# The second product of an MLP's last two token chunks in seven block products of 128x256 instead of eight, after all of the first product

## The chip, the core and the metric

The kernel runs on one core of a Trainium2 chip. Its engines work side by side, each through its own list of instructions in order: TensorE (PE; its weight loads have a row of their own, PEld), VectorE (DVE), ScalarE (ACT), GpSimd (POOL) and SyncE (SP), which here issues nearly all transfers. The metric is the device time of one execution in microseconds, the median of three runs. Products go into eight banks of 128x512 f32 (PSUM); everything else lies in the core's on-chip memory (SBUF) or in the chip's DRAM.

## The reference, cut to what matters

Windowed attention over 8 batches of 8 heads gives x, 4608 tokens of 512 features; an MLP follows. Only the MLP is touched by the change:

```python
h = x @ w_in                                    # 4608x512 by 512x2048
sp = np.maximum(h, 0.0) + np.log1p(np.exp(-np.abs(h)))
g = h * erf(sp)
out = (g @ w_out).astype(np.float32)            # 4608x2048 by 2048x512
```

Every matrix product is made of three: each operand is split into a rounded part (hi) and the rest (lo), and hi by hi, hi by lo and lo by hi are added up in PSUM. Splitting an operand takes a cast (hi, on ACT or DVE) and a subtraction (lo, on DVE).

## The kernel before

The tokens go in nine chunks of 512, the 2048 features of h in eight pairs of 256 (`SPC` is 8, `PAIR` is 2). Chunks 0 to 2 are done plainly, one (chunk, pair) after the other, while most of the attention is still worked off. Chunks 3 to 8 are taken as three couples (`DOUBLES`): for a couple and a pair of features, that is for one d of 0 to 23, h is made by Strassen's seven block products (`mm1_big(d, k)`, k of 0 to 6, L768; six matmuls of 128x512 each, 42 for a d) and `take_big` (L776 to L788) adds each of them into four tiles of 128x512 on DVE: t0 is a copy, t1 to t4 and t6 are additions of 512 columns, t5 one of 1024. The two results of a d are A (the couple's first chunk) and B (its second). They need, in this order, softplus (`argument_big`, L801, ACT), erf (in `period`, L877, ACT) and the product with h (`multiply_big`, L805, DVE). softplus and erf need an ACT table load each time the function changes. B is written to DRAM (`kept_g`) and fetched again later by `load_g`.

The second product is made of items: an item is one chunk's 256 features, (A, d) or (B, d), 24 matmuls of 128x512 (`item_products`, run by `mm`, L636) that add into four banks, `acc`, one per 128 tokens. `split` (L611, L612) makes an item's hi and lo, in halves j of 0 and 1. After the eighth item of a chunk `store` copies the four banks out (L672) and writes them.

This work is laid out by hand in 50 periods, one item in each. In `ITEMS` the items of a couple stand as A of its eight d, then B of its eight d, two periods behind its products. Periods 0 to 7, 16 to 23 and 32 to 39 also hold the 42 products of a d (66 matmuls in all); the other periods have the item's 24 alone. In a period with a d the matmuls go: two block products, six matmuls of the item, two block products, six, two, six, one, six. The block products alternate between two banks, h and tx, so that one product waits until what was in its bank two products earlier has been taken; between the block products the item's matmuls cover that. The order in which an engine gets its instructions is that of the code in `period`; nothing reorders them. `AFT` is a table of small jobs, keyed by period and place (0 to 3) in it; in the periods without a d they build the right-hand sums (`LESS`, `HI`, `LO`) of the next couple. The transfers of a d's left-hand sums (`load_left`, 1.75 MB) alternate between two places in `win`.

## Time and profile before

| | |
|---|---|
| median of three runs | 891.42 us (891.29 to 893.15) |
| the profiled execution: time, span | 892.89 us, 890.9 us |
| granted TensorE clock, mean | 0.996 |
| busy: PE, PEld, DVE, ACT, POOL | 98%, 79%, 71%, 63%, 9% |
| first block product of d = 0, 8, 16 (periods 0, 16, 32) | 354.87, 540.81, 713.14 us |
| bytes moved by DMA | 170.41 MB, 191 GB/s over the span |

A row of a group names the line, the engine, the operation, what it writes and reads, the shape and the count; behind the first bar stand the busy time and the mean length of one in ns, behind the second the time that the engine sat idle just before them and what ended it. A timeline row gives start and length in us and, in brackets, the idle time before it and what ended that. A matmul's or a cast's length there is from its start to its end; the next one of the engine can start before that end. In what follows a "step" of the products of h is the 42 matmuls of one d.

### The profile page before, as it was taken

To read this page: it belongs to the slowest core of one execution; us is meant where nothing else is said; L and a number is where in the kernel's file an instruction comes from. 1 tells how busy PE (TensorE), PEld (TensorE's weight loads), DVE (VectorE), ACT (ScalarE), POOL (GpSimd) and SP (SyncE) were. 2 spreads that over 40 slices of the span, in tenths; PEclk is the share of its full clock that TensorE was granted. 3 is DMA by queue.
4 is the path that set the end of the run, shared out by engine and by line. 5 is a ranking of instruction groups with operands and counts; after the bars stand their busy time and mean duration, and the time that the engine had idled before them with its cause. 6 is when DMAs were issued, how large, how long until landed. Compare 5 with 4: busy or idle time off the path is not lost.

```text
span 890.9 us, 20870 instructions
## 1 busy us (share of the span) xinstructions
PE 871.2 (98%) x8134; PEld 700.1 (79%) x8134; DVE 633.6 (71%) x1575; ACT 564.5 (63%) x1271; POOL 81.3 (9%) x97
## 2 busy tenths in 40 slices
PE   7799999999999999999999999999999999999998
PEld 3367888888888888788887778888888888888886
DVE  5878888987798889777676765666566647576622
ACT  6889888897788886675677442774445434445321
POOL 2312201111111110011000000010000000000000
PEclk9999999999999999999999999999999999999999
DMA  8874446464658896566675741674449125442341
GB/s 272 295 245 154 128 155 197 148 232 127 222 203 270 295 341 248 172 224 221 204 239 200 272 176 54 209 237 161 166 155 361 51 83 200 166 154 83 140 144 48
DMA packets 66915, 170.41 MB, mean 191 GB/s; under 512 B 7680, under 2 KB 14592, under 8 KB 63744
## 3 DMA queue, kind: packets, MB, share of 16 engines
q1 hardware_dynamic: 66528, 168.55, 55.1%
q8 instruction: 64, 1.05, 0.5%
q10 hardware_dynamic: 288, 0.52, 0.2%
q14 instruction: 35, 0.29, 0.1%
HBM read 122.91 MB, written 46.14 MB: 190 GB/s over the span
## 4 chain that ended last, share of the span: by engine, by line
PE 91%; DVE 5%; DMA 1%; ACT 1%; issue 1%; POOL 1%; SPq 0%; DVEq 0%; POOLq 0%; ACTq 0%
PE acc L636 43%; PE h L768 13%; PE tx L768 13%; PE h L521 7%; PE tx L521 7%; PE sp L275 3%; PE sp L217 3%; PE sp L256 1%; PE h L357 1%; DMA qk<-in_qk_dram 1%; DMA v<-in_v_dram 1%; DVE w L458 0%; DVE w L459 0%; DVE prob L228 0%; DVE win L453 0%
## 5 line engine op out<-in xcount | busy, mean ns | idle before, releaser
L636 PE MATMUL acc<-wout_hi,ghi 128*128 128x512 f32 x576 | 227.4, 395 | 0.5 <-DVE ghi L611 0.4
L636 PE MATMUL acc<-wout_lo,ghi 128*128 128x512 f32 x576 | 224.6, 390 | 0.0
L636 PE MATMUL acc<-wout_hi,glo 128*128 128x512 f32 x576 | 159.0, 389 | 0.0
L636 PEld LDWEIGHTS acc<-wout_hi,ghi 128*128 128x128 f32 x576 | 108.2, 188 | 23.3 <-DVE ghi L611 0.9
L636 PEld LDWEIGHTS acc<-wout_hi,glo 128*128 128x128 f32 x576 | 108.1, 188 | 22.8
L636 PEld LDWEIGHTS acc<-wout_lo,ghi 128*128 128x128 f32 x576 | 108.2, 188 | 21.7
L251 POOL TENSOR_TENSOR prob<-prob,rinv 128x256 f32<-128x256 f32 x72 | 72.7, 1016 | 477.0 <-DVE ssum L249 239.9
L238 ACT ACTIVATE prob<-prob,nmax 128x64 f32<-128x64 f32 x288 | 96.3, 338 | 10.5 <-DVE nmax L228 10.3
L801 ACT ACT_TABLE_LOAD x24 | 30.8, 1283 | 93.0 <-DVE dbl L776 47.3
L768 PE MATMUL tx<-win 128*128 128x512 f32 x288 | 74.1, 392 | 0.8 <-DVE hc L778 0.8
L228 DVE CUSTOM_DVE_ANT_0 prob<-sp,cst 128x64 f32<-128x64 f32 x288 | 45.3, 220 | 40.6 <-ACT rows L317 28.2
L768 PE MATMUL h<-win 128*128 128x512 f32 x288 | 74.0, 392 | 0.0
L768 PEld LDWEIGHTS tx<-win 128*128 128x128 f32 x288 | 53.5, 188 | 12.7 <-DVE hc L778 1.2
L768 PEld LDWEIGHTS h<-win 128*128 128x128 f32 x288 | 53.4, 188 | 12.0 <-DVE dbl L778 0.8
L612 DVE TENSOR_TENSOR glo<-hc,ghi 128x512 fp32r<-128x512 f32 x50 | 34.5, 692 | 33.4 <-PE acc L636 22.6
L238 ACT ACTIVATION_READ_ACCUMULATOR prob<-prob,nmax 128x1 f32 x288 | 54.7, 190 | 0.0
L612 DVE TENSOR_TENSOR glo<-dbl,ghi 128x512 fp32r<-128x512 f32 x48 | 33.4, 696 | 28.3 <-PE acc L636 15.6
L521 PE MATMUL h<-x,win 128*128 128x512 f32 x192 | 48.8, 396 | 0.0
L877 ACT ACTIVATE s<-s 128x1024 f32<-128x1024 f32 x48 | 48.2, 1052 | 0.3
L521 PE MATMUL tx<-x,win 128*128 128x512 f32 x192 | 48.0, 392 | 0.0
L801 ACT ACTIVATE s<-hc 128x1024 f32<-128x1024 f32 x24 | 25.5, 1061 | 34.9 <-DVE hc L776 22.8
L611 ACT CAST ghi<-hc 128x512 fp32r<-128x512 f32 x24 | 14.9, 623 | 50.0 <-PE acc L636 41.9
...
## 6 DMA issues: line engine op xcount, KB each, us to landing
...
```

The source lines that it names most:

```text
L217: nc.tensor.matmul(sps[h][r * STRIP:(r + 1) * STRIP, i, p, :], qkz[i][hs, s * STRIP:(s + 1) * STRIP], qkz[i][hs, at:at + KEYS], start=True ...
L228: nc.vector.tensor_tensor_reduce(out=pr[:, g, :], in0=sps[h][:, u % 2, p, :], in1=mask[QUADS.index(kinds(u, p))], scale=-SCALE, scalar=HUG ...
L238: nc.scalar.activation(out=probs[u][:, j, :], in_=probs[u][:, j, :], func=AF.Exp, scale=-1.0, bias=nmax[:, j:j + 1], accum_out=sums[u][:, ...
L251: nc.gpsimd.tensor_tensor(probs[u], probs[u], rinv.broadcast_to([P, 2 * PARTS, KEYS]), op=ALU.mult)
L275: nc.tensor.matmul(xp[h * D:(h + 1) * D, qs], vt[ks, s, h, :], pt[ks, h * P + s * STRIP:h * P + (s + 1) * STRIP], start=True, stop=True, t ...
L521: nc.tensor.matmul((h, bank)[j], win_at[:, ftp, j, cc // 2, w, cc % 2, :], x[cc], start=(k == 0 and i == 0), stop=(k == CC - 1 and i == 2))
L611: (copy or nc.vector.tensor_copy)(out=ghi, in_=e)
L612: nc.vector.tensor_tensor(out=glo, in0=e, in1=ghi.bitcast(F32), op=ALU.subtract)
L636: nc.tensor.matmul(args["out"], args["lhsT"], args["rhs"], start=args["start"], stop=args["stop"])
L768: nc.tensor.matmul(bank_, w[:, wi, c, :], x[c][:, xi, :], start=(c == 0 and n == 0), stop=(c == 1 and n == 2))
L801: nc.scalar.activation(out=ls[kind_, d], in_=hs[kind_, d], func=AF.Softplus)
L877: nc.scalar.activation(out=e, in_=e, func=AF.Erf)
```

## The change

Three things change for the last couple (chunks 7 and 8, d of 16 to 23); everything before period 32 keeps its place.

**The last periods are replaced.** `ITEMS` ends with period 31; its two last items, (B, 14) and (B, 15), are set aside (`REST`). Then `final(d)` makes all of h of the couple, eight steps of 42 matmuls with nothing between them, in four banks (h, tx and the attention's two, sp). A step begins on ACT with both erf of the step before, and t0, the copy, goes to ACT; A is also written to DRAM now (`ga`). `rest_steps` does the two items that were set aside, with the last erf and the last products with h. Then 16 `sums_step`: for chunk 7 and then chunk 8, for each half of its tokens (256), for each quarter of the features (512), the second product is made as seven block products of 128x256: seven products of six matmuls, 42 for a step, that add over the four quarters into seven of the eight banks. After the last quarter `sums_out` adds the seven banks up to the four output blocks and writes them.

**The sums that this needs.** Of g: `row_sums` (four subtractions or additions of 256 columns on DVE) and `operands` (casts on ACT, lo on DVE), made two steps ahead. Of w_out: eight times, p of 0 to 7, `sub_whole` (hi plus lo, two operations of 512 columns on DVE), `sub_sums` (four of 256 columns on DVE, then two casts on ACT) and `sub_split` (two of 512 columns on DVE, four transfers to DRAM, `wd`). Those are put into `AFT` and `LATE`: p = 0 into period 9, p = 5 into periods 11, 13 and 15, p = 1, 2, 3 into periods 20, 21, 22, p = 4 into 23 and 25, p = 6 into 31 and the first step of `final`, p = 7 into its second to fourth. `load_sums` fetches them.

**Small moves.** The loads of the third couple's B11 and B21 go from place 0 of period 24 to its place 3, and in odd d the two tiles that A and B get are swapped.

The counts: 384 matmuls of 128x512 (16 items) become 672 of 128x256, and weights are loaded for each matmul, as before. PE's list has 4134 rows instead of 4150, DVE's 1680 instead of 1548.

```diff
+FIN = DOUBLES - 1
+QUART = SPC // 2
+LASTS = [(kind_, half, q) for kind_ in "AB" for half in range(2) for q in range(QUART)]
...
-        first, then = (("B11", "B21"), ("B12", "B22")) if k == 1 else (("B12", "B22", "B11", "B21"), ())
+        first, then = (("B11", "B21"), ("B12", "B22")) if k == 1 else (("B12", "B22"), ("B11", "B21"))
...
+    SUBS = [lambda p: sub_whole(p), lambda p: sub_sums(p), lambda p: sub_split(p)]
+    for p, places in ((0, ((9, 0), (9, 1), (9, 3))), (1, ((20, 1), (20, 2), (20, 3))), (2, ((21, 1), (21, 2), (21, 3))),
+                      (3, ((22, 1), (22, 2), (22, 3))), (4, ((23, 1), (23, 3), (25, 3))),
+                      (5, ((11, 0), (13, 0), (15, 0))), (6, ((31, 0), (31, 3)))):
+        for sub, (i, q) in zip(SUBS, places):
+            also(i, q, (sub, p))
...
-    ITEMS = [NT - 2, NT - 1] + [(kind_, i * SPC + k) for i in range(DOUBLES) for kind_ in "AB" for k in range(SPC)]
+    ITEMS = [NT - 2, NT - 1] + [(kind_, i * SPC + k) for i in range(FIN) for kind_ in "AB" for k in range(SPC)]
+    ITEMS, REST = ITEMS[:-2], ITEMS[-2:]
+
+    def bank_of(d, k):
+        return (h, bank, *spb)[(7 * d + k) % (4 if d >= FIN * SPC else 2)]
...
         if k == 0:
-            nc.vector.tensor_copy(out=a[:, 1], in_=y)
+            (nc.scalar.copy if d >= FIN * SPC else nc.vector.tensor_copy)(out=a[:, 1], in_=y)
...
-        if kind_ == "B":
-            nc.sync.dma_start(out=kept_g[d // SPC][d % SPC], in_=e)
+        if (kind_, d // SPC) in kept_g:
+            nc.sync.dma_start(out=kept_g[kind_, d // SPC][d % SPC], in_=e)
...
+    def sums_product(s, k):
+        q = s % QUART
+        y, (xh, xl) = bank_at(s, k), operand(s, k)
+        for j in range(2):
+            at_, (wh, wl) = slice(j * P, (j + 1) * P), right(2 * q + j)[k]
+            for n, (x, w) in enumerate(((xh, wh), (xh, wl), (xl, wh))):
+                nc.tensor.matmul(y, x[:, at_], w, start=(q == 0 and j == 0 and n == 0),
+                                 stop=(q == QUART - 1 and j == 1 and n == 2))
...
+    def final(d):
+
+        chain = d > FIN * SPC
+        if chain:
+            for kind_ in "AB":
+                e = ls[kind_, d - 1]
+                nc.scalar.activation(out=e, in_=e, func=AF.Erf)
+        for k in range(4):
+            mm1_big(d, k)
+            take_big(d, k)
+        load_left(NT + d + 2, 0)
+        if chain:
+            multiply_big("A", d - 1)
+        mm1_big(d, 4)
+        take_big(d, 4)
+        jobs(HALFWAY.get(d - FIN * SPC, ()))
+        argument_big("A", d)
+        if chain:
+            multiply_big("B", d - 1)
+        for k in (5, 6):
+            mm1_big(d, k)
+            take_big(d, k)
+        argument_big("B", d)
+        load_left(NT + d + 2, 1)
+        jobs(LATE.get(d - FIN * SPC, ()))
+
+    LATE = {0: [(sub_split, 6)], 1: [(sub_whole, 7)], 2: [(sub_sums, 7), (load_e, 0, room_halves)],
+            3: [(sub_split, 7)], 4: [(row_sums, 0, room_w)], 5: [(operands, 0, 0), (operands, 0, 1)],
+            6: [(operands, 0, 2), (operands, 0, 3), (load_rest,), (load_sums, 0), (load_sums, 1)],
+            7: [(load_e, 1, lambda: slab(1)), (load_sums, 2)]}
+    HALFWAY = {7: [(split_rest, 0, 0), (split_rest, 0, 1)]}
...
+    def sums_step(s):
+        last_ = s % QUART == QUART - 1
+        for g, ks in enumerate(GROUPS):
+            for k in ks:
+                sums_product(s, k)
+            if s == 0 and g == 0:
+                operands(1, 3)
+            if g == 0:
+                row_sums(s + 2, room_s)
+            if last_:
+                for k in ks:
+                    sums_out(s, k)
+            operands(s + 2, g)
+        load_e(s + 4, lambda: room_e(s + 4))
+        if s < 2:
+            load_sums(6 + s)
...
+        for d in range(FIN * SPC, DOUBLES * SPC):
+            final(d)
+        rest_steps()
+        for s in range(len(LASTS)):
+            sums_step(s)
```

How the lists of instructions change at three places (dbl_ and hc are tiles of h, s the tiles of softplus and erf; the new lines are those of the changed kernel). **ACT, from d = 18 to d = 19**, before and then after:

```order
L801 ACTIVATE s<-dbl_8622 128x1024
L801 ACTIVATE s<-dbl_8623 128x1024
L877 ACT_TABLE_LOAD
L877 ACTIVATE s<-s 128x1024 x2
L801 ACT_TABLE_LOAD
L801 ACTIVATE s<-hc 128x1024 x2
```

```order
L821 ACTIVATE s<-hc 128x1024 x2
L1135 ACT_TABLE_LOAD
L1135 ACTIVATE s<-s 128x1024 x2
L798 COPY dbl_8667<-sp_90 128x512
L821 ACT_TABLE_LOAD
L821 ACTIVATE s<-dbl_8667 128x1024
L821 ACTIVATE s<-dbl_8668 128x1024
```

The second list is from d = 17 to d = 18: the copy t0 of a new step (L798) now stands on ACT, behind the softplus and both erf of the step before. **DVE, the step d = 18 of the changed kernel**, which starts with t1:

```order
L796 TENSOR_TENSOR dbl_8667<-sp_91,dbl_8667 128x512
L796 TENSOR_TENSOR dbl_8668<-h,dbl_8667 128x512
L796 TENSOR_TENSOR dbl_8668<-tx,dbl_8668 128x512
L825 TENSOR_TENSOR hc<-hc,s 128x1024
L796 TENSOR_TENSOR dbl_8667<-sp_90,dbl_8668 128x512
L825 TENSOR_TENSOR hc<-hc,s 128x1024
L808 TENSOR_TENSOR dbl_8668<-sp_91,dbl_8668 128x1024
L796 TENSOR_TENSOR dbl_8668<-h,dbl_8668 128x512
```

The split of items (L616, L617), which stood among these rows, is gone; t1 reads the tile that ACT's copy wrote. **DVE, period 21 (d = 13)**, before and after:

```order
L778 COPY hc<-tx 128x512
L776 TENSOR_TENSOR hc<-h,hc 128x512
L776 TENSOR_TENSOR hc<-tx,hc 128x512
L776 TENSOR_TENSOR hc<-h,hc 128x512
L805 TENSOR_TENSOR dbl_7713<-dbl_7713,s 128x1024
L611 CAST ghi<-dbl_7713 128x512
L612 TENSOR_TENSOR glo<-dbl_7713,ghi 128x512
L776 TENSOR_TENSOR hc<-tx,hc 128x512
L788 TENSOR_TENSOR hc<-h,hc 128x1024
L805 TENSOR_TENSOR dbl_7714<-dbl_7714,s 128x1024
L776 TENSOR_TENSOR hc<-tx,hc 128x512
```

```order
L798 COPY hc<-tx 128x512
L796 TENSOR_TENSOR hc<-h,hc 128x512
L796 TENSOR_TENSOR hc<-tx,hc 128x512
L796 TENSOR_TENSOR hc<-h,hc 128x512
L950 TENSOR_TENSOR rows<-wout_hi,wout_lo 128x512 x2
L825 TENSOR_TENSOR dbl_7747<-dbl_7747,s 128x1024
L616 CAST ghi<-dbl_7747 128x512
L617 TENSOR_TENSOR glo<-dbl_7747,ghi 128x512
L950 TENSOR_TENSOR rows<-rows 128x256 x4
L796 TENSOR_TENSOR hc<-tx,hc 128x512
L808 TENSOR_TENSOR hc<-h,hc 128x1024
L825 TENSOR_TENSOR dbl_7748<-dbl_7748,s 128x1024
```

Six operations (L950) stand ahead of t4, which is the next to last L796 row. **DVE and ACT, period 9 of the changed kernel**, where chunk 3 ends and p = 0 is built:

```order
L617 TENSOR_TENSOR glo<-hc,ghi 128x512
L950 TENSOR_TENSOR s<-wout_hi,wout_lo 128x512 x2
L950 TENSOR_TENSOR s<-s 128x256 x4
L617 TENSOR_TENSOR glo<-dbl_6633,ghi 128x512
L677 COPY o<-acc_93 128x512
L677 COPY w<-acc_95 128x512
```

```order
L974 CAST s<-s 128x512 x2
L616 CAST ghi<-dbl_6633 128x512
L677 COPY w<-acc_94 128x512
L677 COPY w<-acc_96 128x512
L616 CAST ghi<-dbl_6633 128x512
```

The copies that free the banks acc (L677; L672 before) now stand behind the L950 rows on DVE and behind two casts of p's sums (L974) on ACT; before, neither was there.

More of the change, by code (lines that the diff above doesn't have):

```diff
@@ L771, in take_big @@
     def take_big(d, k):
-        y = (h, bank)[(7 * d + k) % 2]
+        y = bank_of(d, k)
         if k == 0:
@@ L794, in pair_of @@
         if d % 2:
-            return [work.tile([P, PAIR, TOK], F32, name="hc") for _ in range(2)]
+            return [work.tile([P, PAIR, TOK], F32, name="hc") for _ in range(2)][::-1]
         return [slab(i) for i in range(2)]
@@ new lines, in sub_whole, with sub_sums @@
+    def sub_whole(p):
+        subs[p] = sub_room(p)
+        for j, r in enumerate(subs[p][0]):
+            less(r, wout_hi[:, 2 * p + j, :].bitcast(F32), wout_lo[:, 2 * p + j, :].bitcast(F32), ALU.add)
+    def sub_sums(p):
+        (b11, b12), (b21, b22) = [(t[:, 0:HN], t[:, HN:TOK]) for t in subs[p][0]]
+        less(b11, b12, b11)
+        less(b12, b22, b12)
+        less(b22, b22, b11)
+        less(b21, b22, b21)
+        for r, hi in zip(*subs[p]):
+            nc.scalar.copy(out=hi, in_=r)
@@ new lines, in right, with load_e @@
+    def right(p):
+        w11, w12, w21, w22 = ([w[:, 2 * p + j, n * HN:(n + 1) * HN] for w in (wout_hi, wout_lo)]
+                              for j in range(2) for n in range(2))
+        return w11, w21, sum_at(p, 1, 1), sum_at(p, 0, 1), sum_at(p, 0, 0), w22, sum_at(p, 1, 0)
+    es, rs, ops = {}, {}, {}
+    GROUPS = ((0, 1), (2, 3), (4, 5), (6,))
+    def load_e(s, room):
+        if s < len(LASTS):
+            kind_, half, q = LASTS[s]
+            es[s] = room()
+            for k in range(2):
+                to = es[s][k] if isinstance(es[s], list) else es[s][:, k].rearrange("p (j n) -> p j n", j=PAIR)
+                nc.sync.dma_start(out=to,
+                                  in_=kept_g[kind_, FIN][2 * q + k][:, :, half * HN:(half + 1) * HN])
@@ new lines, in room_e, with parts_of, row_sums @@
+    def room_e(s):
+        return work.tile([P, PAIR, TOK], F32, name="hc") if s % 2 else slab(1 - s // 2 % 2)
+    def parts_of(s):
+        view = "p k (j r n) -> p k j r n"
+        if isinstance(es[s], list):
+            return [(slice(k, k + 1), t.rearrange("p (k j) (r n) -> p k j r n", k=1, r=2))
+                    for k, t in enumerate(es[s])]
+        return [(slice(0, 2), es[s].rearrange(view, j=PAIR, r=2))]
+    def row_sums(s, room):
+        if s < len(LASTS):
+            r = rs[s] = room()
+            for ks, e in parts_of(s):
+                a11, a12, a21, a22 = (e[:, :, j, n, :] for n in range(2) for j in range(PAIR))
+                s2, s3, s1, s4 = (t.rearrange("p (n k m) -> p n k m", n=2, k=2)[:, n, ks]
+                                  for t in r for n in range(2))
+                less(s1, a21, a22, ALU.add)
+                less(s2, s1, a11)
+                less(s3, a11, a21)
+                less(s4, a12, s2)
@@ new lines, in room_s, with op_room @@
+    def room_s():
+        t = work.tile([P, PAIR, TOK], F32, name="s")
+        return [t[:, 0], t[:, 1]]
+    def op_room(s):
+        if s % 2 == 0:
+            return [work.tile([P, S], F32R, name="rows", bufs=4)[:, 0:TOK] for _ in range(4)] + [
+                one.tile([P, QW + KW], F32R, name=f"qk{i}")[:, 0:TOK] for i in range(2)] + [
+                one.tile([P, TOK], F32R, name="v0")]
+        wide = [io.tile([P, PAIR, TOK], F32R, name=n, bufs=1) for n in ("plain", "dbl2")]
+        return [w[:, j] for w in wide for j in range(PAIR)] + [
+            one.tile([P, TOK], F32R, name="v1"), one.tile([P, TOK], F32R, name="pT1"),
+            work.tile([P, TOK], F32R, name="ghi")]
```

136 lines of the change are left out of this document (133 added, 3 removed).

## The prediction

> **What bounds the kernel now.** I read the page's busy times and its chain of waits first, then busy times by stretch, then timelines of single engines at the places that change.
>
> ```profile
> PE 871.2 (98%) x8134; PEld 700.1 (79%) x8134; DVE 633.6 (71%) x1575; ACT 564.5 (63%) x1271; POOL 81.3 (9%) x97
> ...
> PE 91%; DVE 5%; DMA 1%; ACT 1%; issue 1%; POOL 1%; SPq 0%; DVEq 0%; POOLq 0%; ACTq 0%
> ```
>
> The chain that ended last is PE for 91%: what counts is how many matmuls there are, at what pace, and where they wait. By stretch (engines' busy us, then granted clock, DMA share and GB/s):
>
> ```profile
> 497.30:502.00 4.70, 4.26 (x20) 3.22 (x18) 2.09 (x3) 3.75 (x4) 0.00 (x0) 1.00 0.99 363
> ...
> 609.64:654.60 44.96, 44.96 (x205) 37.25 (x199) 28.39 (x38) 20.44 (x25) 0.00 (x0) 1.00 0.46 160
> ...
> 713.14:832.80 119.66, 119.66 (x529) 99.10 (x528) 75.73 (x102) 51.60 (x49) 0.00 (x0) 1.00 0.38 132
> ```
>
> The last row covers the eight steps of h that the change rebuilds: PE is never idle there, and DVE (75.7 of 119.7) and ACT (51.6) have room, because each step also holds an item. The pace and the end, from PE's timeline (the last row is ACT's issue of a transfer):
>
> ```profile
> 873.62 0.39 PE L636 MATMUL acc<-wout_hi,ghi 128*128 128x512 f32 x1
> ...
> 876.34 0.39 PE L636 MATMUL acc<-wout_hi,ghi 128*128 128x512 f32 x1
> ...
> 886.99 0.39 PE L636 MATMUL acc<-wout_hi,glo 128*128 128x512 f32 x1
> ...
> 888.03 0.34 ACTq L674 DMA_DIRECT2D out_dram<-w  x1
> ```
>
> Twelve matmuls lie between the first two rows: 2.72 / 12 = 0.2267 us each. From 713.14 to the end there are 8 x 42 + 18 x 24 = 768 of them, 174.1 us, up to 887.25; the last copy and transfer take 3.65, which gives the span of 890.9. That stretch of 177.8 us is what I cost anew.
>
> **The products of 128x256.** They remove 384 matmuls (87.05 us) and add 672 of half the length, each with weights of its own. What weights cost shows where PE had stood still, and in the steady stream:
>
> ```profile
> 483.57 0.76 PEld L768 LDWEIGHTS tx<-win 128*128 128x128 f32 x4 [1.21 <-DVE hc L778]
> 483.57 0.96 PE L768 MATMUL tx<-win 128*128 128x512 f32 x3 [0.79 <-DVE hc L778]
> ...
> 879.06 0.39 PE L636 MATMUL acc<-wout_hi,ghi 128*128 128x512 f32 x1
> 879.06 0.19 PEld L636 LDWEIGHTS acc<-wout_lo,ghi 128*128 128x128 f32 x1
> ```
>
> Three matmuls after the stall took 0.96; 2 x 0.2267 + 0.39 is 0.84, so the first waited about 0.11 for its weights. In the stream a load starts together with the matmul before it (879.06), so it is hidden. Bounds for a matmul of 256 columns: half of 0.2267, 0.113, if the loads of 0.11 stay just hidden; 0.113 + 0.11 = 0.223, if nothing overlaps at this length. The stream's row is nearest to the lower one; I take 0.120, since no room is left over the loads. 672 x 0.120 = 80.6: **6.4 us less** (bounds 11 less, 63 more). The Trainium skill (TensorE: Matmul & The Clock Gate, Back-to-back issue gap) puts a lone matmul at its columns over 2.4 GHz plus 2.5 ns, 109 ns here; by that estimate the 672 take 73 us and the saving is 14. For 512 columns the same rule gives 216 ns where this trace shows 227, so I stay with the row.
>
> **The chain through final.** In a step PE needs 42 x 0.2267 = 9.52 us. But t0 is now ACT's, behind both erf of the step before; these wait for that step's softplus of B, this for its t6, and t6 stands last on DVE, behind the rest of the step. So ACT's stretch and DVE's follow one another. Before, the same pieces show at d = 15 (DVE, then ACT, then PE):
>
> ```profile
> 663.02 0.69 DVE L776 TENSOR_TENSOR hc<-tx,hc 128x512 f32<-128x512 f32 x1 [0.67 <-PE tx L768]
> 663.63 1.22 DVE L805 TENSOR_TENSOR dbl<-dbl,s 128x1024 f32<-128x1024 f32 x1
> 664.95 0.43 DVE L611 CAST ghi<-dbl 128x512 fp32r<-128x512 f32 x1
> ...
> 666.09 1.22 DVE L805 TENSOR_TENSOR dbl<-dbl,s 128x1024 f32<-128x1024 f32 x1
> 667.23 1.22 DVE L788 TENSOR_TENSOR hc<-h,hc 128x1024 f32<-128x1024 f32 x1
> 668.55 0.69 DVE L776 TENSOR_TENSOR hc<-tx,hc 128x512 f32<-128x512 f32 x1
> ...
> 672.80 1.22 DVE L805 TENSOR_TENSOR hc<-hc,s 128x1024 f32<-128x1024 f32 x1 [2.28 <-ACT s L877]
> ```
> ```profile
> 669.33 1.06 ACT L801 ACTIVATE s<-hc 128x1024 f32<-128x1024 f32 x1 [3.39 <-DVE hc L776]
> 670.41 1.28 ACT L877 ACT_TABLE_LOAD   x1
> 671.71 2.01 ACT L877 ACTIVATE s<-s 128x1024 f32<-128x1024 f32 x2
> ```
> ```profile
> 675.06 0.39 PE L636 MATMUL acc<-wout_hi,ghi 128*128 128x512 f32 x1
> ...
> L593 ACT COPY hc<-h 128x512 f32<-128x512 f32 x8 | 4.5, 566 | 0.0
> ...
> L611 ACT CAST ghi<-hc 128x512 fp32r<-128x512 f32 x24 | 14.9, 623 | 50.0 <-PE acc L636 41.9 <-DMA hc<-g 6.7 <-issue 1.4
> ```
>
> ACT's part: t6 ends at 669.24; softplus, table load and the two erf (started 0.95 apart) let the copy start at 673.6; with its 0.57 and, as from t6 to softplus, 0.09 to reach DVE that is 5.0 after t6. DVE's part: an operation of 512 columns lets the next start after 0.61 (663.02 to 663.63), one of 1024 after 1.14 (666.09 to 667.23); one that needs the result before it starts some 0.10 after its end (1.32 from 667.23 to 668.55). t1 0.61, t2 0.79, t3 0.61, product A 1.14, t4 0.61, product B 1.14, t5 1.32, t6 0.69: 6.9. A step takes **11.9 instead of 9.5**; there are seven such passages: 7 x 2.4 = 16.9 us. Four banks don't help: PE's fifth product waits for the bank that this copy empties, and PE stands still some 2.4 us per step.
>
> Jobs that lie in the chain: after d = 18 two casts on ACT wait for four small DVE operations (priced below: 1.8, then 1.2 for the casts, 1.1 of it hidden by softplus): 1.9. After d = 21 casts of 512 and twice 256 columns, 1.2, and after d = 22 of 512 and twice 128, 1.1 (estimates from the cast's 0.62). In d = 23 two lo's ahead of product B, 2 x 0.61 = 1.2. Together 5.4. The other jobs of LATE run on DVE while it waits for ACT, 5 us each time, and cost nothing; in a chain without that wait they would cost 1.2 to 2.4 each.
>
> Ends: t6 of the first step lies 0.9 behind PE (0.2 and 0.69). After the last t6, (B, 15) needs its hi, cast behind both erf: 5.1; then 24 matmuls, 5.44, with about 0.5 for its second half's lo, which stands behind two products of h: 11.0. Item (B, 14) fits into the wait.
>
> The sums: a step of 42 takes PE 5.04. DVE does about 1.5 for row_sums and 2.2 for lo's, made two steps ahead, and 4.2 more, nine additions, in each fourth step: 19.0 per four steps against PE's 20.2. ACT needs 2.3 of 5.04. I cost this at nothing; at the pace of 0.113 (19.0) DVE would just set it. Transfers: 2.75 MB per step of final over 11.9 us, 231 GB/s, and some 17 MB in the 90 us behind it, against 363 in the first stretch row: hidden.
>
> From 713.14: 76.2 + 0.9 + 16.9 + 5.4 + 11.0 + 80.6 + 3.65 = 194.7 instead of 177.8: **+16.9**.
>
> **The small jobs ahead of it.** What an operation of 256 columns costs, and period 21 (DVE; PE):
>
> ```profile
> 340.71 0.41 DVE L540 TENSOR_TENSOR dbl<-dbl 128x256 f32<-128x256 f32 x1
> 341.16 0.42 DVE L541 TENSOR_TENSOR dbl<-dbl 128x256 f32<-128x256 f32 x1
> 341.62 0.43 DVE L542 TENSOR_TENSOR dbl<-dbl 128x256 f32<-128x256 f32 x1
> ...
> 634.81 0.68 DVE L776 TENSOR_TENSOR hc<-tx,hc 128x512 f32<-128x512 f32 x1
> ```
> ```profile
> 636.98 0.84 PE L768 MATMUL tx<-dbl,win 128*128 128x512 f32 x3
> ```
>
> Four of 256 in a row take 4 x 0.46 = 1.84, two of 512 1.22. In period 21 all six stand ahead of t4 (634.81), which would end at 638.56; k6 needs t4's bank and was due at 636.98: 1.6 late, and the same in periods 20 and 22: 4.8. In period 23 t6 (668.55) comes 1.2 later, then sub_sums and two casts stand ahead of erf's table load on ACT: product A at 675.9 instead of 672.80, and its item on PE at 677.7 instead of 675.06: 2.6. Period 9:
>
> ```profile
> 504.29 0.69 DVE L612 TENSOR_TENSOR glo<-hc,ghi 128x512 fp32r<-128x512 f32 x1
> 505.08 0.69 DVE L612 TENSOR_TENSOR glo<-dbl,ghi 128x512 fp32r<-128x512 f32 x1
> 505.71 0.69 DVE L672 COPY o<-acc 128x512 f32<-128x512 f32 x1
> ```
> ```profile
> 507.55 0.39 PE L636 MATMUL acc<-wout_hi,ghi 128*128 128x512 f32 x1
> ...
> 524.00:529.50 5.50, 5.50 (x26) 4.53 (x26) 3.95 (x8) 1.73 (x4) 0.00 (x0) 1.00 0.43 161
> ```
>
> The sums end at 508.0, two casts on ACT at 508.7, the next item's hi behind them at 509.3, its lo at 510.1 and only then the copy that frees the first bank, at 510.7. PE wants that bank at 507.55: 3.2. p = 5 and 6 stand in periods of the last row's kind, DVE 3.95 of 5.50 us: nothing, about 1 each if that room is gone. Sum: **+10.6**.
>
> **The rivals.** (1) The small jobs are covered: DVE has 16.6 of 45 us free in periods 20 to 22 (second stretch row), more than the 3 x 4.28 = 12.8 that is added. Against it: in a list that is worked off in order the place decides, not the sum. 908. (2) Faster: ACT's and DVE's stretches overlap after all, so that a step ends within PE's 9.52; then 76.2 + 0.9 + 11.0 + 80.6 + 3.65 = 172.4, 5.4 less than before, 886 with the jobs covered. It decides, with all other jobs covered, from passages under 10.3 us on. Only each engine's own sum speaks for it (7 us per step on either); the copy's place behind the erf speaks against it. (3) Weights are not hidden at 256 columns: 672 x 0.223, 69 us more, 988. The loads' start with the matmul before speaks against it. (4) TensorE's clock falls in the gaps:
>
> ```profile
> 8.00:13.00 5.00, 2.90 (x41) 1.28 (x40) 1.97 (x11) 2.82 (x15) 0.83 (x2) 0.83 0.95 314
> ...
> 366.00:370.00 4.00, 2.47 (x14) 1.81 (x12) 3.34 (x7) 0.73 (x1) 0.00 (x0) 1.00 0.01 4
> ```
>
> Idle for 2.1 of 5 us the clock was 0.83, 0.85 us lost; idle for 1.5 of 4 it stayed 1.00. Within final PE has 2.4 us per step to lose; behind the 4.6 us before (B, 15) it hasn't: 1 to 2 us, 921. The Trainium skill (TensorE: Matmul & The Clock Gate, HAM oscillation) has the clock halve after an idle window of about 3.4 us; only that last gap and those behind the added casts are as long.
>
> **How the numbers follow.** 16.9 + 10.6 = 27.5: the profiled execution, 892.89 (span 890.9 and 2.0 around it), would become 920.4. The median lies 1.47 below it, 891.42, so I forecast **919**. Chances: this 0.66, (1) 0.15, (2) 0.08, (3) 0.03, (4) 0.05, and 0.03 that errors of both signs leave no change. Its own range is 912 to 925 (pace 0.113 takes 4.7 off, DVE-bound sums and 3 us of stalls add). With (1) at the lower pace 903, and with (4) and late transfers 927: 903 to 927. Some 0.2% is what a measurement of this kernel can tell from no change: faster 0.09, within it 0.03, slower 0.88.
>
> **What would show it.** In the changed profile: steps of L788 11.9 us apart with PE idle 2 to 4 us in each, behind ACT's L798; L1091 at 0.120 per matmul without gaps; PE waiting for DVE in period 9 (3 us), before k6 in 20 to 22, and in 25. Steps 9.5 us apart would prove the forecast wrong, and so would L1091 at 0.2.

## The result, and the profile after

The changed kernel takes **933.85 us** (median of 5 runs, 930.65 to 935.84) against 892.60 of the kernel before beside it (5 runs, 891.29 to 893.80): a ratio of **1.0463, 95% interval 1.0435 to 1.0491**. The forecast was 919, range 903 to 927: the direction was right, the time 7 us outside the range. The profiled execution took 930.65 (span 928.9), 37.8 more than the profiled one of before.

Busy times and the chain of waits, on the page after:

```profile
PE 875.0 (94%) x8410; PEld 714.3 (77%) x8422; DVE 698.8 (75%) x1747; ACT 601.7 (65%) x1347; POOL 80.1 (9%) x97
...
PE 75%; DVE 11%; ACT 5%; DMA 5%; issue 3%; POOL 0%; SPq 0%; DVEq 0%; ACTq 0%; POOLq 0%
```

PE's share of the chain fell from 91% to 75%; DVE, ACT and DMA took its place. By stretch of the changed kernel (from d = 12 to 15; d = 15 to 16; d = 16 to the first product of the sums; their first four steps; the other twelve), columns as in the prediction:

```profile
611.26:661.15 49.89, 45.91 (x205) 37.04 (x199) 38.15 (x59) 23.83 (x30) 0.00 (x0) 1.00 0.56 181
661.15:722.83 61.68, 59.40 (x259) 48.19 (x258) 46.38 (x74) 28.94 (x42) 0.00 (x0) 1.00 0.59 205
722.83:831.65 108.82, 92.70 (x385) 73.52 (x384) 68.14 (x98) 65.15 (x73) 0.00 (x0) 0.97 0.70 238
831.65:865.26 33.61, 24.86 (x170) 24.45 (x168) 19.36 (x48) 10.06 (x22) 0.00 (x0) 0.80 0.79 286
865.26:925.61 60.35, 60.35 (x506) 60.35 (x504) 45.69 (x103) 23.29 (x43) 0.00 (x0) 1.00 0.32 104
```

The last row is what was forecast for all of the sums: 504 products in 60.35 us, 0.120 each, PE never idle. The row above it was not: four steps, 168 products, 20.2 us at that pace, took 33.6, and the granted clock was 0.80. What PE waited for there, and further back in final (PE's waits from 800 on: us in total, times, longest):

```profile
PE sp L1091 <- DMA win<-wd: 8.7, 2, 6.5
PE acc L641 <- ACT ghi L616: 3.3, 1, 3.3
PE sp L788 <- ACT dbl L798: 3.2, 1, 3.2
PE tx L788 <- ACT hc L798: 1.3, 1, 1.3
```

The first row is a transfer: w_out's sums, loaded into win's cells, came late. SP's own list of issues shows why (start, time to issue; below them the wait of SP that stands in the gap, and count, size and median us to landing of these loads):

```profile
823.75 1.18 SPq L1007 DMA_DIRECT2D dbl<-ga  x2
825.02 1.02 SPq L987 DMA_DIRECT2D win<-wd  x2
827.49 0.32 SPq L828 DMA_DIRECT2D ga<-hc  x1
828.62 0.32 SPq L828 DMA_DIRECT2D g<-hc  x1
835.56 1.18 SPq L1007 DMA_DIRECT2D hc<-ga  x2
836.83 2.04 SPq L987 DMA_DIRECT2D win<-wd  x4
...
SPq L1007 <- DMA g<-hc: 6.6, 1, 6.6
...
win<-wd SPq DMA_DIRECT2D x16, 512.0 KB, 7.6
```
```profile
845.11 2.29 PE L1091 MATMUL sp<-win,dbl 128*128 128x256 f32 x9 [6.46 <-DMA win<-wd]
...
860.42 1.42 PE L1091 MATMUL sp<-win,dbl 128*128 128x256 f32 x9 [2.28 <-DMA win<-wd]
```

From 828.94 to 835.56 SP stood still: the left side of step 2 (L1007) goes into the buffer whose store (828.62) had not landed. The weights of p = 3 and 4 stand behind it and are issued at 836.83, 20 us after the last product of h (816.55), though their cells were empty by then; loads of this kind land a median 7.6 us after their issue. Step 1 wanted p = 3 at 838.6 and went on at 845.1 (PE's first row); step 3 waited in the same way for p = 7.

The chain through final went as forecast. DVE, ACT and PE around d = 18:

```profile
744.35 0.69 DVE L796 TENSOR_TENSOR hc<-tx,hc 128x512 f32<-128x512 f32 x1
...
750.02 0.69 DVE L796 TENSOR_TENSOR dbl<-sp,dbl 128x512 f32<-128x512 f32 x1 [3.77 <-ACT dbl L798]
...
756.21 0.69 DVE L796 TENSOR_TENSOR dbl<-h,dbl 128x512 f32<-128x512 f32 x1
```
```profile
745.14 1.06 ACT L821 ACTIVATE s<-hc 128x1024 f32<-128x1024 f32 x1 [0.72 <-DVE hc L796]
746.22 1.28 ACT L1135 ACT_TABLE_LOAD   x1
747.51 2.00 ACT L1135 ACTIVATE s<-s 128x1024 f32<-128x1024 f32 x2
749.42 0.56 ACT L798 COPY dbl<-sp 128x512 f32<-128x512 f32 x1
```
```profile
750.04 3.02 PE L788 MATMUL sp<-x,win 128*128 128x512 f32 x12 [2.04 <-ACT dbl L798]
763.10 2.93 PE L788 MATMUL tx<-x,win 128*128 128x512 f32 x6 [3.25 <-ACT hc L798]
```

From t6 to t6 it is 11.86 us: 4.98 from the end of t6 to the start of t1 (ACT's part, forecast 5.0) and 6.88 of DVE's work (forecast 6.9). DVE waits 3.77 for ACT's copy, which stands behind both erf, and PE 2 to 3 us for the bank that the copy empties.

### The profile page after: what moved, and what is told of

The parts are those of the page before. It is cut to its first block, busy times and chain, and to the rows that moved or that the text cites. A ratio compares the mean times of both kernels' runs of the same rounds, so it can differ in the third digit from the quotient of the medians.

```text
span 928.9 us, 21935 instructions
## 1 busy us (share of the span) xinstructions
PE 875.0 (94%) x8410; PEld 714.3 (77%) x8422; DVE 698.8 (75%) x1747; ACT 601.7 (65%) x1347; POOL 80.1 (9%) x97
## 4 chain that ended last, share of the span: by engine, by line
PE 75%; DVE 11%; ACT 5%; DMA 5%; issue 3%; POOL 0%; SPq 0%; DVEq 0%; ACTq 0%; POOLq 0%
PE acc L641 28%; PE h L788 8%; PE tx L788 8%; PE h L526 7%; PE tx L526 6%; PE acc L1091 3%; PE sp L280 3%; PE sp L222 3%; DMA win<-wd 2%; PE sp L1091 2%; DVE hc L796 2%; ACT s L1135 2%; DVE rows L950 1%; PE sp L261 1%; DVE dbl L796 1%
## 5 line engine op out<-in xcount | busy, mean ns | idle before, releaser
L641 PE MATMUL acc<-wout_hi,ghi 128*128 128x512 f32 x448 | 178.1, 398 | 8.7 <-ACT ghi L616 4.0
L641 PE MATMUL acc<-wout_lo,ghi 128*128 128x512 f32 x448 | 174.8, 390 | 0.0
L641 PE MATMUL acc<-wout_hi,glo 128*128 128x512 f32 x448 | 123.9, 390 | 0.1
L641 PEld LDWEIGHTS acc<-wout_hi,ghi 128*128 128x128 f32 x448 | 84.2, 188 | 28.1 <-ACT ghi L616 5.2
L641 PEld LDWEIGHTS acc<-wout_hi,glo 128*128 128x128 f32 x448 | 84.1, 188 | 18.4 <-DVE glo L617 0.5
L641 PEld LDWEIGHTS acc<-wout_lo,ghi 128*128 128x128 f32 x448 | 84.2, 188 | 16.6
L233 DVE CUSTOM_DVE_ANT_0 prob<-sp,cst 128x64 f32<-128x64 f32 x288 | 45.2, 220 | 38.3 <-ACT rows L322 27.6
L788 PE MATMUL tx<-win 128*128 128x512 f32 x240 | 62.1, 394 | 1.6 <-DVE hc L798 1.6
L788 PE MATMUL h<-win 128*128 128x512 f32 x240 | 61.9, 393 | 0.0
L788 PEld LDWEIGHTS tx<-win 128*128 128x128 f32 x240 | 44.4, 188 | 12.1 <-DVE hc L798 2.4
L788 PEld LDWEIGHTS h<-win 128*128 128x128 f32 x240 | 44.4, 188 | 10.2 <-DVE dbl L798 0.7
L322 ACT COPY rows<-sp 128x128 f32<-128x128 f32 (+7 forms) x167 | 27.6, 309 | 27.9 <-PE sp L222 27.4
L821 ACT ACTIVATE s<-dbl 128x1024 f32<-128x1024 f32 x24 | 25.4, 1060 | 27.8 <-DVE dbl L796 27.7
L821 ACT ACTIVATE s<-hc 128x1024 f32<-128x1024 f32 x24 | 25.5, 1061 | 27.5 <-DVE hc L796 19.0
L526 PEld LDWEIGHTS h<-x,win 128*128 128x128 f32 x192 | 35.4, 188 | 8.0
L526 PEld LDWEIGHTS tx<-x,win 128*128 128x128 f32 x192 | 35.7, 188 | 7.5
```

Source lines behind the costliest of these rows:

```text
L233: nc.vector.tensor_tensor_reduce(out=pr[:, g, :], in0=sps[h][:, u % 2, p, :], in1=mask[QUADS.index(kinds(u, p))], scale=-SCALE, scalar=HUG ...
L322: nc.scalar.copy(out=to, in_=src)
L526: nc.tensor.matmul((h, bank)[j], win_at[:, ftp, j, cc // 2, w, cc % 2, :], x[cc], start=(k == 0 and i == 0), stop=(k == CC - 1 and i == 2))
L641: nc.tensor.matmul(args["out"], args["lhsT"], args["rhs"], start=args["start"], stop=args["stop"])
L788: nc.tensor.matmul(bank_, w[:, wi, c, :], x[c][:, xi, :], start=(c == 0 and n == 0), stop=(c == 1 and n == 2))
L821: nc.scalar.activation(out=ls[kind_, d], in_=hs[kind_, d], func=AF.Softplus)
```

## The experiments

The starts of the first products give the stretches of every run (us; "h" is product d's first L788, "sums" from the first to the last of their products). Each ratio is to the kernel before, run beside it on the same chip, with its 95% interval.

| kernel | d 7-8 | d 12-13 | d 15-16 | d 16-23 | d 23-sums | sums | median | ratio |
|---|---|---|---|---|---|---|---|---|
| before | 61.1 | 15.1 | 58.5 | - | - | - | 892.6 | 1 |
| changed | 64.9 | 16.7 | 61.7 | 82.8 | 26.0 | 94.0 | 933.9 | 1.0463 |
| copy_first | 66.8 | 16.8 | 61.7 | 70.9 | 26.2 | 95.1 | 922.9 | 1.0325 (1.0293-1.0357) |
| t0_dve | 65.5 | 16.7 | 61.7 | 69.5 | 26.4 | 94.6 | 924.1 | 1.0359 (1.0336-1.0383) |
| places | 60.4 | 15.1 | 62.5 | 81.2 | 27.6 | 93.4 | 924.9 | 1.0354 (1.0330-1.0379) |
| skip | 65.6 | 16.7 | 61.7 | 81.2 | 27.7 | 90.0 | 930.9 | 1.0415 (1.0392-1.0439) |
| early | 64.8 | 16.7 | 61.7 | 81.2 | 27.6 | 91.4 | 930.8 | 1.0415 (1.0391-1.0438) |
| direct | 65.4 | 16.7 | 61.7 | 81.2 | 30.0 | 80.5 | 922.4 | 1.0332 (1.0312-1.0352) |
| all | 60.8 | 15.1 | 64.9 | 68.8 | 23.8 | 83.4 | 900.9 | 1.0085 (1.0066-1.0104) |
| all2 | 64.6 | 15.1 | 59.5 | 74.9 | 20.7 | 90.5 | 908.9 | 1.0187 (1.0161-1.0213) |
| all3 | 60.5 | 15.1 | 60.7 | 66.7 | 20.4 | 86.9 | 894.5 | 1.0016 (1.0004-1.0028) |
| all4 | 61.1 | 15.1 | 61.0 | 66.6 | 20.4 | 90.0 | 896.6 | 1.0055 (1.0038-1.0072) |
| all5 | 60.6 | 15.1 | 60.2 | 67.3 | 20.4 | 87.2 | 895.0 | 1.0034 (1.0021-1.0048) |
| all6 | 61.0 | 15.1 | 60.3 | 67.1 | 20.4 | 85.5 | 894.5 | 1.0024 (1.0008-1.0041) |

**copy_first: the place of t0's copy.**

```diff
-        if chain:
-            for kind_ in "AB":
-                e = ls[kind_, d - 1]
-                nc.scalar.activation(out=e, in_=e, func=AF.Erf)
         for k in range(4):
             mm1_big(d, k)
             take_big(d, k)
+            if chain and k == 0:
+                for kind_ in "AB":
+                    e = ls[kind_, d - 1]
+                    nc.scalar.activation(out=e, in_=e, func=AF.Erf)
```

> Edit: in each step of final after the first, ACT copies t0 ahead of the two erf of the step before, not behind them. Theory of the chain (ACT's and DVE's stretches follow one another because t0 stands behind both erf): from t6 to t1 there are then only softplus and the copy, some 1.8 us instead of 5.0, the passage falls to about 9 us, below PE's 9.52, and seven steps take 66.6 instead of the 82.8 us of the changed kernel's trace (first product of d = 16 to first product of d = 23): 16 us less, about 917 for the whole, less what the loads of the sums give back if they are late again. Rival (DVE's own work, or PE's banks, set the step): the steps stay between 11 and 12 us and the time within 3 us of the changed kernel's 933.9.

The seven steps fell by 11.9 us, to 70.9; the rival's 11 to 12 us a step is out. Three steps are 9.52, PE's own, the others 10.0 to 11.8, so that it is 11.9 and not 16. In the longest, ACT's copy waits for a store from the same buffer to land:

```profile
782.33 0.58 ACT L798 COPY hc<-sp 128x512 f32<-128x512 f32 x1 [3.33 <-DMA ga<-hc]
```

The sums stayed at 95: the loads were late in the same way (PE waited 11.8 us for win<-wd).

**t0_dve: the same from the other side.**

```diff
-            (nc.scalar.copy if d >= FIN * SPC else nc.vector.tensor_copy)(out=a[:, 1], in_=y)
+            nc.vector.tensor_copy(out=a[:, 1], in_=y)
```

> Edit: t0 in final is copied by DVE again, as before the change; both erf stay first in each step. Theory (the chain runs through ACT's copy, which stands behind both erf): with the copy on DVE t0 to t3 run while ACT does softplus, table load and erf; product A then starts some 3.5 us after t6 and the passage takes 3.5 + 1.14 + 0.61 + 1.14 + 1.32 + 0.69 = 8.4 us, below PE's 9.52; without jobs the steps are 9.5 us long, seven steps take 67 to 72 instead of 82.8, though DVE has 0.6 us more to do in each: 11 us less or more, about 922. Rival (erf first is itself what lengthens the step, or DVE's own work sets it): the steps stay at 11 us or more, and the time within 4 us of the changed kernel's 933.9.

Steps of 9.5 to 10.6 with both erf still first and more work on DVE: neither "erf first" nor DVE's own sum set the step, but ACT's copy behind the erf.

**places: the small jobs.**

```diff
-    for p, places in ((0, ((9, 0), (9, 1), (9, 3))), (1, ((20, 1), (20, 2), (20, 3))), (2, ((21, 1), (21, 2), (21, 3))),
-                      (3, ((22, 1), (22, 2), (22, 3))), (4, ((23, 1), (23, 3), (25, 3))),
-                      (5, ((11, 0), (13, 0), (15, 0))), (6, ((31, 0), (31, 3)))):
+    for p, places in ((0, ((9, 3), (10, 1), (11, 0))), (1, ((20, 1), (20, 3), (21, 1))), (2, ((21, 3), (22, 3), (23, 1))),
+                      (3, ((22, 1), (24, 3), (25, 3))), (4, ((26, 1), (28, 1), (30, 1))),
+                      (5, ((13, 0), (14, 0), (15, 0))), (6, ((31, 0), (31, 3)))):
```

> Edit: the small jobs that build w_out's sums go to other places of the list: p = 0 from period 9 to 9, 10 and 11; p = 1, 2, 3 and 4 no longer three to one period in 20 to 23, but one to a half period from 20 to 30; p = 5 one each in 13, 14 and 15. The work is the same. Theory (the place decides, not the sum of DVE's work): the periods between first products of d = 12 and d = 15 go back from 16.6 to 15.0 us each, d = 7 to 8 from 64.9 to about 61, d = 15 to 16 from 61.7 to about 58.5; 9 to 11 us less, about 924. Rival (DVE has no room for 4.3 us more per period wherever they stand): the delay goes with the jobs to the new periods, d = 7 to d = 16 stays within 3 us of the changed kernel's 245.3 us, and the time does too.

d = 7 to 8 takes 60.4 us again, and d = 12 to 15 runs at 15.0 per period. More than half of the work that was added in the latter stretch stays there (DVE's busy time was 28.39 us before, 38.15 in the changed kernel, and is 34.16 here), and PE doesn't wait for it:

```profile
608.72:653.74 45.02, 45.02 (x205) 37.27 (x199) 34.16 (x50) 21.25 (x26) 0.00 (x0) 1.00 0.52 177
```

So the place decides; the run all3 (below) keeps 36.9 us of DVE's work in this stretch, and PE doesn't wait there either. d = 15 to 16 got no better: the jobs moved to periods 23 to 25 delay two items there (PE waits 1.5 us for DVE's ghi).

**skip: what are the waits for weights worth?**

```diff
-                load_sums(3)
...
-        if s < 2:
+        if s < 1:
             load_sums(6 + s)
```

> Edit: the loads of w_out's sums for p = 3 and p = 7 are left out, so the products of those two read what lies in the cells and two eighths of the last two chunks are not the reference's; number and shape of all other instructions stay. Theory (transfers): step 1 of the sums no longer waits 7.0 us and step 3 no longer 2.7 us for their weights, the half clock behind the waits goes too, and the sums take 81 to 83 us instead of 94.0 (first product of the sums to the last): about 921. Rival (the queue: whatever is next in SP's list is late, since SP stands still for 6.6 us at a transfer that waits for another to land): the waits move to p = 2, to p = 6 or to the left sides, the sums take 88 us or more, and the time stays within 5 us of the changed kernel's 933.9.

The numbers are the rival's (sums 90.0, the time 3 us less), the place isn't. Steps 1 and 3 lost their waits, but step 2 now waits for its own weights, p = 4 and 5, which had been there in time when step 1 was late (PE's waits in the sums):

```profile
PE sp L1091 <- DMA win<-wd: 6.3, 2, 4.3
```

**early: all weights ahead of the entry that blocks.**

```diff
-            7: [(load_e, 1, lambda: slab(1)), (load_sums, 2)]}
+            7: [(load_sums, 2), (load_sums, 3), (load_e, 1, lambda: slab(1)), (load_sums, 4), (load_sums, 5),
+                (load_sums, 6), (load_sums, 7)]}
...
-                load_sums(3)
...
-        load_sums(4)
...
-        load_sums(5)
...
-        if s < 2:
-            load_sums(6 + s)
```

> Edit: the loads of w_out's sums for p = 2 to 7 are all issued behind the last product of h, ahead of SP's entry that waits for stores of g to land; the same bytes, another order. Theory of the queue: p = 3 and p = 7 arrive before steps 1 and 3 want them, the 9.7 us of waits for weights go, and the sums take 81 to 85 us instead of 94.0; up to 4 us may come back at step 2, since its left side is loaded later: about 920 to 925. Rival (bandwidth: the transfers cannot go faster than the 395 to 411 GB/s of the densest stretches): the same bytes are late in another place, waits of 7 us or more stay in the first four steps, and the time stays above 929.

No wait for weights is left. But the left side of step 2 is late instead, because its buffer's store now stands behind 4 MB of weights (PE's waits in the sums, then SP's list):

```profile
PE h L1091 <- ACT rows L1068: 6.2, 1, 6.2
```
```profile
834.70 0.32 SPq L828 DMA_DIRECT2D g<-hc  x1
844.67 1.18 SPq L1007 DMA_DIRECT2D hc<-ga  x2
```

Again the numbers are the rival's: the waits of PE in the sums come to 8.1 us, and the time is 930.8. Moving one load only makes another late. What helps must load less, or earlier.

**direct: another order of d, so that less is wanted at once.**

```diff
-LASTS = [(kind_, half, q) for kind_ in "AB" for half in range(2) for q in range(QUART)]
+LASTS = [(kind_, half, q) for kind_ in "AB" for half in range(2) for q in (0, 3, 1, 2)]
...
-    ROOM = ((7, 8), (9, 14), (0, 1), (2, 3), (4, 5), (6, 15), (10, 11), (12, 13))
+    ROOM = ((7, 8), (9, 14), (4, 5), (6, 15), (10, 11), (12, 13), (0, 1), (2, 3))
...
-                es[3] = [hs["A", i][:, :, 0:HN] for i in (d - 1, d)]
-                load_e(2, lambda: work.tile([P, PAIR, TOK], F32, name="hc"))
+                es[1] = [hs["A", i][:, :, 0:HN] for i in (d - 1, d)]
+                load_e(2, lambda: slab(1))
```

> Edit: the second step of the sums takes d = 22 and 23, whose left sides still lie on chip and need no load, and the order of d in the eight groups follows (0, 3, 1, 2); w_out's sums for the first two steps go to the cells that the products of d = 23 leave first, and the loads of p = 6, 7, 2 and 3 are issued during and right behind these products; the later left sides go to buffers whose stores landed earlier. The same products, the same bytes but one left side. Theory (what is needed first was loaded last, in a queue that is worked off in order): no wait for weights or left sides is left in the first four steps, the half clock goes too, and the sums take 81 to 83 us instead of 94.0, first product to last; final is as in the changed kernel; about 921. Rival (bandwidth: between the last product of h and step 3 there are more bytes than the 395 to 420 GB/s of the densest stretches can bring): 5 us or more of waits stay in steps 1 to 3, and the time stays above 927.

```profile
836.91:917.42 80.51, 80.51 (x672) 80.51 (x671) 61.46 (x142) 31.74 (x63) 0.00 (x0) 1.00 0.45 156
```

All 672 products at 0.120, clock 1.00, no wait: the forecast 80.6. By the ratios the time fell by 11.7 us against the changed kernel, though the way from d = 16 to the sums became 2.4 us longer; there the granted clock was 0.50 from 827.8 to 834.5, behind the 3.3 us in which PE waits for the hi of (B, 15), while in the changed kernel it stayed at 1.00 behind the same wait. That settles the missing 13.4 us: late transfers and the slower clock behind the waits, not the products.

**all: everything together**, copy_first, direct and other places of the small jobs; ACT's casts ("h") now run from a list BEHIND, worked off after the two erf, DVE's part ("l") stays in LATE.

```diff
+    BEHIND = {3: [(sub_sums, 7)], 5: [(operands, 0, 0, "h"), (operands, 0, 1, "h")],
+              6: [(operands, 0, 2, "h"), (operands, 0, 3, "h")]}
...
+                jobs(BEHIND.get(d - FIN * SPC, ()))
...
+        if d == DOUBLES * SPC - 1:
+            nc.scalar.activation(out=ls["A", d], in_=ls["A", d], func=AF.Erf)
```

> Edit: everything together: t0's copy ahead of the erf, the small jobs spread (nothing in periods 23 to 26 but one in 26), the loads and the order of d as in the run before last, ACT's casts for jobs of final placed behind the erf and DVE's part behind t6, and in the rest the hi of (B, 15) is cast ahead of softplus of B. Theory (chain, small jobs and late loads are all that made the change slow): steps of final 9.5 us, d = 16 to the start of the sums 87 to 89 us instead of 108.8, the sums 81 to 82, the products of d = 8 to 16 at the periods of the kernel before; the span becomes 713.1 + 88 + 81.5 + 3.3 = 886, the time 888, or 0.5% faster than before (0.9945). Rival (something of the changed work cannot be hidden: DVE's sums or the transfers): the steps stay above 10 us or the sums above 85, and the time is above 895, slower than before.

copy_first, places and direct by themselves took 1.38, 1.09 and 1.31 points off the ratio, together 3.78; all, which holds some smaller edits too, takes 3.78 off. With intervals of 0.2 to 0.3 points on each, that they agree to two digits is luck, but the three causes add up. Neither theory nor rival came out whole: the steps are 9.5 to 10.9, the sums 83.4, and yet 7.6 us remain: d = 15 to 16, jobs in final, the rest, and 2.8 us in the sums.

**all2** put right what was late in all, and broke something else. Beside other places of the small jobs and of some loads its core is, against all:

```diff
-        load_left(NT + d + 2, 0)
...
         if chain:
             multiply_big("A", d - 1)
+        load_left(NT + d + 2, 0)
```

> Edit: as the run called all, with what its trace showed to be late put right: the small jobs go where DVE and ACT both stand idle (sums of p = 2 and 3 behind the first products of periods 22 and 23; p = 4 joins p = 0 and 5 in periods 9 to 15; p = 6 into the first steps of final); the store of product A goes ahead of the next load of w_in's sums, of d = 22 and 23 only the half is stored that is read again; the left side of the rest is loaded ahead of w_out's sums, and p = 3 to 5 later. Theory (the 8 us by which all is slower than before are 6.4 from d = 15 to d = 16, 2.2 in final, 2.6 ahead of the rest and 2.8 in the sums, each a thing that came late at its place): d = 15 to 16 takes 58.5 to 59.5 us, the seven steps 67 to 68, from d = 23 to the first product of the sums 20.5 to 21.5 instead of 23.8, the sums 81 to 83; the time is 887 to 890, 0.3 to 0.7% faster than before. Rival (the transfers around the end of h are at their limit, since these 35 us move some 13 MB, 385 GB/s): what is loaded earlier makes something else late, the stretch from d = 23 to the end of the sums stays within 2 us of the 107.1 of the run all, and the time is not below 893.

d = 15 to 16 and d = 23 to the sums came out as expected, the sums got worse, p = 4 and 5, now both in periods 11 to 15, cost 3.9 us (d = 7 to 8), and in final every step from d = 18 to 22 waited 2.0 to 4.2 us for a store, which now stood behind a megabyte of w_in's sums (DVE):

```profile
778.20 0.69 DVE L796 TENSOR_TENSOR hc<-tx,hc 128x512 f32<-128x512 f32 x1 [4.15 <-DMA g<-hc]
```

**all3**: both stores ahead of both loads, and the other moves that the expectation names, against all2:

```diff
         if chain:
             multiply_big("A", d - 1)
-        load_left(NT + d + 2, 0)
...
             multiply_big("B", d - 1)
+        load_left(NT + d + 2, 0)
```

> Edit: as the run called all2, but p = 4 goes back to periods 26 to 30 and p = 6 into the first step of final; both stores of a step of final go ahead of both loads of w_in's sums (in all2 the first load stood between them, and DVE waited 2.0 to 4.2 us per step for the store of product B to land); p = 3 and 4 are loaded ahead of, and the output of the rest stored behind, the left sides of steps 2 and 3. Theory (what all and all2 still lose is order in SP's queue and places of jobs): d = 7 to 8 takes 60.5 to 61 us, d = 15 to 16 58.5 to 60, the seven steps 66.6 to 68.5, d = 23 to the sums 20.5 to 21.5, the sums 80.5 to 82.5; the time is 886 to 890, 0.3 to 0.8% faster than before (0.992 to 0.997). Rival (transfers at their limit: final moves 2.75 MB per 9.5 us and the 31 us behind it some 11 MB, in whatever order): two or more of these stretches stay 2 us or more above their values, and the time is 893 or more.

Final is now at PE's own pace, seven steps in 66.7 (7 x 9.52), and the way from d = 23 takes 20.4. The sums stay at 86.9; there the rival is right. PE's waits in them are 3.0 us; another 2.7 go to 29 products at half pace, since the granted clock is 0.50 from 814.8 to 821.6:

```profile
714.43:781.12 66.69, 66.69 (x296) 55.17 (x294) 52.74 (x77) 48.58 (x54) 0.00 (x0) 1.00 0.79 287
790.41:801.52 11.11, 11.11 (x51) 9.20 (x49) 8.21 (x18) 10.33 (x13) 0.00 (x0) 1.00 1.02 405
801.52:888.46 86.94, 83.96 (x673) 83.35 (x671) 64.70 (x146) 33.12 (x66) 0.00 (x0) 0.96 0.49 174
```

**all4, all5, all6** changed only the order of the loads (first line, all4), then the queue of some loads and stores (the next two, all5; the last, all6), each against the one before.

```diff
+            7: [(load_e, 2, lambda: slab(1)), (load_sums, 2), (load_sums, 3)]}
...
+            queue = nc.gpsimd if d >= DOUBLES * SPC - 2 else nc.sync
...
+                (nc.gpsimd if s in (2, 3) else nc.sync).dma_start(out=to,
...
+            (nc.gpsimd if c == NCH - 3 else nc.sync).dma_start(out=out[r:r + P, :], in_=o)
```

> Edit: as the run called all3, but in SP's queue the left side of step 2 goes ahead of w_out's sums for p = 2 and 3, and these ahead of p = 4 (in all3 the left side was issued last, landed 9.5 us later behind 4.5 MB, and steps 1 and 2 of the sums took 6.8 and 9.1 us instead of 5.04); the same instructions, the same bytes, only this order. Theory (each load in time if the queue holds them in the order in which PE wants them; 12 MB in 35 us are within the 400 GB/s of the stretch): all steps of the sums but the first take 5.04 us, the sums 80.6 to 82 instead of 86.9, and the time is 887 to 890, 0.3 to 0.7% faster than before. Rival (bandwidth): some step is late in any order, the sums stay at 84 us or more, and the time is 892 or more, no faster than before.

> Edit: as the run called all4, but the stores of d = 22 and 23 and the left sides of steps 2 and 3 are issued by POOL, in a queue of its own, and SP's queue holds only w_out's sums behind the loads of the rest; the same transfers and bytes. Theory of the queue (in all4 SP stood still from 795 to 801 for a store that landed 9.5 us after it was issued, and the next left side landed 11.4 us after its issue, each behind the megabytes ahead of it in the one queue): with a second queue the stores land in 3 to 5 us, SP never waits, the sums of the weights are all issued by about 806, the sums take 80.6 to 82.5 us instead of 90.0 (all3 86.9), and the time is 887 to 890, 0.3 to 0.7% faster than before. Rival (bandwidth: some 12 MB in 30 us is all that the engines move, whatever the queue): the left sides share the rate and are late as before, the sums stay at 85 us or more, the time at 892 or more.

> Edit: as the run called all5, but the four stores of the output that stands ahead of the sums go to POOL's queue too, so that in SP's queue the left sides of steps 4 and 5 stand right behind the last of w_out's sums (in all5 they stood behind these stores, which took 5 us to issue, and step 4 of the sums waited for its left side: steps 3 and 4 took 6.2 and 10.0 us). Theory (only the order was left to put right): the steps are 5.04 us but for the first, the sums 81 to 82.5 us instead of 87.2, and the time is 888.5 to 891, 0.2 to 0.5% faster than before. Rival (the engines run at 410 to 429 GB/s from 787 to 815 without a gap, and what is late is what was put last): the left side of step 4 or 5 stays late, the sums stay above 85 us, and the time at 893 or more.

All three theories failed. Each time what was put last was late: in all4 the left side of step 3 (PE waits 3.2 us for what is made of it), in all5 that of step 4, in all6 weights of step 3 (1.1 us) and again the left side of step 4 (DVE waits 2.6 us for it, PE 1.5 for DVE). GB/s in all6 from 787 to 815, in 40 slices:

```profile
GB/s 272 219 179 199 284 307 316 316 351 386 439 404 433 392 433 410 427 410 433 410 439 398 416 415 427 415 421 416 416 421 416 421 421 421 416 421 427 398 398 427
```

From the eleventh slice on it is 392 to 439 without a gap, 418 on average, stores included. A step of the first four wants four loads of 512 KB and two of 256 KB, 2.62 MB (the one whose left side is on chip 2.10); in 5.04 us 2.62 MB is 520 GB/s. So the loads can't keep pace with these steps: what is not there when the sums start is in danger of coming late, and in the orders tried some of it did. The run direct, with the same order of d, had no wait: its way from d = 23 to the sums is 9.6 us longer, which at this rate is 4 MB. all4 lost time to the queue as well: SP stood still 5.6 us for a store, and from 800 to 810 the rate was 252. Whether another order would fit isn't shown.

The Trainium skill (DMA: Bandwidth & Descriptors, Specifications) puts the ceiling of the SBUF ports at 435 GB/s, and (Issuing engines are not separate DMA queues) says that DMAs issued by different engines run on the same 16. The traces agree with both: 418 is the average here, and single slices of 0.7 us, 439 at most in all6 and 445 in all5, lie 1 to 2% above the ceiling; a second queue kept SP from standing still for a store, but added no rate (on average from 787 to 815: 385 in all3 with one queue, 386 in all5 and 384 in all6 with two).

None of these versions beats the kernel before; all3 is 0.16% slower (0.04 to 0.28).

## Why the prediction was wrong

**"Transfers ... hidden" failed.** That step set 17 MB in the 90 us behind final against a rate of 363 GB/s. The bytes are not wanted over 90 us: 7.3 MB of the loads that are issued behind the last product of h (six p of 1.05, two left sides of 0.52) are wanted in the first four steps of the sums, and SP's queue held them behind entries that waited for stores. It costs 13.4 us (94.0 instead of 80.6), of which 9.1 are two gaps of PE and some 4 the clock behind them (43 products at 0.213 us instead of 0.120):

```profile
840.00:845.00 5.00, 0.00 (x0) 0.00 (x0) 4.84 (x14) 2.68 (x6) 0.00 (x0) 0.61 0.93 266
845.00:850.00 5.00, 4.89 (x23) 4.89 (x24) 1.99 (x6) 0.79 (x2) 0.00 (x0) 0.50 1.04 411
850.00:855.00 5.00, 5.00 (x39) 5.00 (x39) 1.96 (x6) 1.46 (x4) 0.00 (x0) 0.87 1.03 393
...
860.00:865.00 5.00, 4.58 (x25) 4.58 (x26) 3.13 (x8) 1.34 (x3) 0.00 (x0) 0.66 0.33 117
```

PE is busy from 845 to 850, but with 23 products instead of 42. How the 13.4 us divide between the queue that stood still and the rate isn't shown; direct shows that both together cost them. The forecast had late transfers only in the range's upper end, together with rival (4), at 927. Rival (4) had the mechanism, but in another place: it expected the clock to fall behind the wait ahead of (B, 15), for 1 to 2 us. That happened in direct, not in the changed kernel's trace. The 3.4 us of idle time by which the prediction picks its gaps isn't what the traces show: 2.3 us were enough ahead of 860.42, and 2.0 in skip. In final the clock was 0.50 twice, from 762.6 to 766.0 and from 800.2 to 803.5 (the six products at 763.10 take 2.93, nearly as long as the twelve at 750.04). It cost nothing there: in skip, where the clock fell in other steps, each of the seven stretches from t6 to t6 is as long as here within 0.01, since the chain goes through DVE and ACT.

**The pace, 0.120 per product of 256 columns, was right** (80.51 for 672 in direct), so rival (3) is out and the products save their 6.4 us.

**The chain was right**, cause and size: 11.86 us a step against 11.9; from d = 16 to the sums 108.8 against 110.4. Its jobs were priced a little high: d = 18 cost 1.2, not 1.9. copy_first and t0_dve show ACT's copy behind the erf as its cause.

**The small jobs were right**, in place and nearly in size: 1.6 in each of periods 20 to 22 as forecast, 3.8 instead of 3.2 for period 9, 3.2 instead of 2.6 for periods 23 to 25; 11.9 in all against 10.6. PE waits where it was said, for the copy that frees a bank in period 9, for t4's bank in 20 to 22, and for an item's hi in the last stretch:

```profile
PE acc L641 <- DVE o L677: 2.8, 1, 2.8
...
PE h L788 <- DVE dbl L796: 2.7, 2, 1.3
PE tx L788 <- DVE hc L796: 1.3, 1, 1.3
...
PE acc L641 <- DVE ghi L616: 1.4, 1, 1.4
```

Rival (1) is out as a forecast for this list, though places and all3 show that its room was there.

**Rival (2)**, steps within 9.52, is what all3 reaches. Its 886 was too low for the same reason as the forecast: the transfers come late in the sums.

The sum for the profiled execution, 27.5, then becomes 27.5 + 13.4 (sums) + 1.3 (jobs) - 1.6 (chain) - 0.4 (end) = 40.2; the stretch ahead of d = 7 was 2.2 shorter by chance, 38.0 against 37.8 measured. The shift to the median went the other way: the profiled execution lies 3.2 below its median, the one of before 0.3 above that of the five runs, so that the medians stand 41.3 apart.
